# A second batch loaded as pairs of heads in six-token runs, with a recomputed order

## The chip, the cores and the metric

The kernel runs on one core of a Trainium2 chip. The metric is the device time of one execution in microseconds (us): the median of 4 runs before the change is 292.82 us, from 292.14 to 293.37. Engines are named as in the profile: PE is TensorE (PEld its weight loads), DVE VectorE, ACT ScalarE, POOL GpSimd, SP SyncE.

## What is computed

Causal attention over 8 batches and 8 heads, with 16 beacon keys in front of 576 keys, followed by a multiplicative feed-forward network over all 4,608 tokens.

```python
k_all = np.concatenate([beacon_k, k], axis=2)      # B, H, 16 + 576, 64
v_all = np.concatenate([beacon_v, v], axis=2)
scores = scale * np.matmul(q, k_all.transpose(0, 1, 3, 2))
scores = np.where(causal, -1000000000.0, scores)
a = np.exp(scores - scores.max(-1, keepdims=True))
a /= a.sum(-1, keepdims=True) + 1e-09
x = np.matmul(a, v_all)            # then tokens x (heads * 64) = 4608 x 512
out = ((x @ w1) * (x @ w2) @ w3) @ w_out    # d_ff = 1024
```

Inputs and output are float32; the kernel computes in fp16 with float32 sums.

## The kernel before

**The order.** The whole program is one string, `ORDER`: a list of small operations that a planner has put in an order for all engines at once. Each operation is a Python function of the same name (the table `ops` at the end). Every engine and every DMA queue executes its own part of the list in list order, and semaphores make it wait for what it needs. So the place of an operation in the list sets what it queues behind. The digits behind an operation are the batch, the chunk or head pair, and at the end the PSUM bank; A or D is the engine that copies, ScalarE or VectorE; P, S or A behind a load or store is the queue, POOL, SyncE or ScalarE.

**Loads.** Nearly all loads go through POOL's queue, which converts float32 to fp16 on the way: `lq`, `lk`, `lv` (q, k, v of a batch in five chunks `0` to `4` of up to 128 token rows, lines 332 and 340), `lkb`, `lvb` (beacons), `l1`, `l2` (column blocks of w1 and w2, line 390), `l3` (row blocks of w3, line 399) and `lo` (w_out, line 402). An unpaired chunk comes with tokens on partitions and heads side by side, so that every piece is one token of one head, 64 values.

Batch 0 comes otherwise (line 349): `lq 0 c` and `lk 0 c` load a *pair of heads*, `c` from 0 to 3, with six consecutive tokens on each of 96 partitions, so a piece is 6 x 64 values. Such a load lands in half of a buffer of the output staging `st8`; `cast` (line 407) moves it to `o16` in an order fit for TensorE, `tq`/`tk` (line 418) make six transposes of 96 x 96 in place of four per chunk, and `eq`/`ek` (line 437) copy the result from PSUM to `qTs`/`kTs`. The beacons of batch 0 go by way of `tn` and `en`.

**Transposing the rest.** For other batches a chunk of q or k is transposed either by TensorE (`tq`/`tk`, then `eq`/`ek`) or by a DMA transpose on SyncE's queue (`Dq` at line 471, `Dk` at line 477). Buffers of q, k, v, qT and kT exist twice, by batch number modulo 2.

**Attention.** `s b g` computes one of 13 groups of score blocks of batch b into a pair of PSUM banks (line 508). Group 0 needs the last query chunk and all keys. `exp` (ScalarE, line 518) writes them to a ring of 8 buffers; `m` masks on VectorE; `v` multiplies by the values (line 539) and `n` divides by the sums (VectorE). `x`/`ex` on TensorE, or `TX` as a DMA transpose on SyncE (line 574), put the result into `xT`.

**Feed-forward.** w3 is folded into w_out once, in the first third of the loads: `t3`, `e3`, `f`, `ew` make `Wt = w3 @ w_out`, with `t3` and `f` on TensorE (lines 484 and 493). For each of nine stretches of 512 tokens, `a` and `b` (line 580) are the products with 128 columns of w1 and w2, four matmuls each; `ea` and `eb` multiply them; `o` (line 601) are eight matmuls with `Wt`; `eo` copies and `st` stores. `a m f` needs the w1 block `f // 2`, loaded by `l1`, and `b m f` that of w2, loaded by `l2`. `spin` is idle work that keeps TensorE running.

Of the kernel before, what the change touches and what calls it, by code (L numbers as in the profile page):

```python
# [74 lines left out]
f 1 3 6; lv 1 0; ek 0 2 D 5; tk 1 0 7; ew 1 A 6; f 5 0 4; ek 1 0 D 7; l3 7; tq 0 3 5; f 5 1 4;
l2 1; eq 0 3 D 5; f 5 2 4; cast 0 2 q A; lq 1 1 P; f 5 3 4; tq 0 2 6; ew 5 A 4; lv 1 4; tk 1 1 7;
eq 0 2 D 6; ek 1 1 A 7; tk 1 2 5; l1 2; ek 1 2 D 5; s 0 6 0; s 0 7 2; lq 1 3 P; exp 0 6 0;
tq 1 4 6; v 0 1 0 7; eq 1 4 D 6; v 0 0 1 5; lk 1 4 P; n 0 1 0 7; exp 0 7 2; v 0 0 0 6; lq 1 0 P;
n 0 0 1 5; s 0 8 0; s 0 9 2; s 0 10 4; n 0 0 0 6; exp 0 8 0; lk 1 3 P; v 0 1 1 7; m 0 2 0; t3 7 6;
exp 0 9 2; m 0 2 1; l1 0; s 0 11 0; e3 7 D 6; exp 0 11 0; v 0 2 0 3; lvb 1; n 0 1 1 7; f 7 0 6;  # L80
lkb 2; tq 1 1 2; exp 0 10 4; n 0 2 0 3; s 0 12 0; f 7 1 6; m 0 3 0; f 7 2 6; m 0 3 1; eq 1 1 A 2;
lq 2 0 P; v 0 3 0 7; exp 0 12 0; v 0 2 1 5; lv 1 3; n 0 3 0 7; tq 1 3 4; tk 1 4 3; n 0 2 1 5;
x 0 0 7; eq 1 3 A 4; l1 1; v 0 3 1 2; ek 1 4 A 3; ex 0 0 D 7; f 7 3 6; lv 1 1; n 0 3 1 2; tq 1 0 7;
ew 7 A 6; tk 1 3 5; l2 0; x 0 4 4; eq 1 0 D 7; x 0 2 3; ek 1 3 A 5; x 0 3 6; ex 0 4 D 4; x 0 1 7;
ex 0 3 D 6; ex 0 2 A 3; lv 1 2; s 1 0 0; s 1 1 4; s 1 2 2; ex 0 1 D 7; exp 1 0 0; a 0 4 6; l1 3;
exp 1 1 4; m 1 0 0; l2 2; a 0 0 7; ea 0 4 D 6; l2 3; exp 1 2 2; tq 2 0 5; m 1 0 1; a 0 5 6;
# [104 lines left out]
def kernel(  # L191
# [13 lines left out]
    nc = tc.nc  # L205
# [492 lines left out]
```

## Time and profile before

| what | value |
|---|---|
| median of 4 runs | 292.82 us (292.14 to 293.37) |
| the profiled execution | 293.16 us |
| its span, first to last instruction | 291.5 us |
| TensorE clock granted | 0.999 |
| POOL's DMA queue | 114,960 packets, 26.98 MB |
| SyncE's and ScalarE's DMA queue | 40,016 packets, 11.40 MB |
| HBM read, written | 39.32 MB, 9.44 MB |
| pair load of batch 0 on POOL | 6 of them, 0.64 to 0.67 us to issue |
| chunk load of q, k or v on POOL | mean 0.86 us to issue |

How to read it: the page gives each engine's busy time and its share of the span, and then the span in 40 equal slices of 7.3 us, one digit each (9 is 90% busy or more). The row `DMA` is the mean over the core's 16 DMA engines. The *chain of waits* goes back from the last instruction, at each step to what released it. *Landing* is the moment when a DMA's data are there. Packets under 512 bytes are 145,136 of 155,214.

### The profile page before, as it was taken

What the parts mean: (1) busy time and instruction counts of PE and PEld (TensorE: products, weight loads), DVE (VectorE), ACT (ScalarE), POOL (GpSimd) and SP (SyncE); (2) the same over time, 40 slices, a digit from 0 to 9 for tenths busy, and PEclk for the clock granted to TensorE, in tenths of its full rate; (3) what the DMA queues carried; (4) which work ended last, traced back from release to release, by engine and by line L of the source; (5) the groups of instructions that cost most, each with busy time, mean ns of one, the idle gap of its engine ahead of it and who ended that gap; (6) DMA issues with size and microseconds to landing.
All of it is one profiled execution on the core that took longest, in us unless ns stands there. A gap on an engine that the chain in (4) does not pass through costs nothing.

```text
span 291.5 us, 6996 instructions
## 1 busy us (share of the span) xinstructions
PE 282.8 (97%) x2894; PEld 153.1 (53%) x2894; DVE 169.2 (58%) x366; ACT 148.6 (51%) x190; POOL 135.5 (46%) x189
## 2 busy tenths in 40 slices
PE   6999999999999999999999999999999999999995
PEld 3445674566565555565444554555555544444443
DVE  4435684874576668765573665447655566562660
ACT  3834888177926865766205573587255741002002
POOL 8768979786984752754582810591010000100000
PEclk9999999999999999999999999999999999999999
DMA  8999999999999999999999990699951111043003
GB/s 164 196 191 178 176 157 174 165 137 150 184 162 130 197 167 173 142 148 155 173 195 156 213 125 18 115 169 153 155 145 45 38 27 38 36 103 133 0 36 144
DMA packets 155214, 39.10 MB, mean 134 GB/s; under 512 B 145136, under 2 KB 151024, under 8 KB 155184
## 3 DMA queue, kind: packets, MB, share of 16 engines
q0 software_dynamic: 114960, 26.98, 106.5%
q1 hardware_dynamic: 40016, 11.40, 26.0%
q8 instruction: 22, 0.36, 0.5%
q10 hardware_dynamic: 208, 0.29, 0.4%
q14 instruction: 8, 0.07, 0.1%
HBM read 39.32 MB, written 9.44 MB: 167 GB/s over the span
## 4 chain that ended last, share of the span: by engine, by line
PE 76%; DMA 13%; POOL 7%; issue 1%; ACT 1%; SPq 0%; DVE 0%; POOLq 0%; ACTq 0%
PE one L580 40%; PE one L601 21%; PE one L539 8%; PE pair L508 7%; DMA w<-in_moe_w_dram 5%; DMA xT<-x 3%; DMA xT<-in_moe_w_dram 3%; DMA wo<-in_moe_w_out_dram 2%; POOL va L340 2%; POOL w L390 1%; ACT ring L518 1%; POOL st L357 1%; POOL q L332 1%; POOL xT L399 1%; POOL k L340 1%
## 5 line engine op out<-in xcount | busy, mean ns | idle before, releaser
L580 PE MATMUL one<-xT,w 128*128 128x512 f16 x576 | 134.6, 380 | 1.0 <-DMA w<-in_moe_w_dram 0.8
L518 ACT ACTIVATE ring<-pair 128x1024 f16<-128x1024 f32 x104 | 99.1, 1027 | 30.2 <-PE pair L508 29.8
L580 PEld LDWEIGHTS <-w 128*128 128x128 f16 x576 | 52.7, 98 | 60.1 <-issue 2.6
L601 PE MATMUL one<-Wt,gT 128*128 128x512 f16 (+1 forms) x296 | 66.5, 374 | 0.0
L595 DVE TENSOR_TENSOR gT<-one,asb 128x512 f16<-128x512 f32 x72 | 49.1, 689 | 21.8 <-PE one L580 15.0
L615 POOL DMA_DIRECT2D out_dram<-st x29 | 16.5, 569 | 92.4 <-ACT st L300 49.1
L300 ACT ACTIVATE asb<-one 128x512 f32<-128x512 f32 x36 | 21.4, 604 | 59.2 <-DVE gT L595 28.2
L601 PEld LDWEIGHTS <-gT 128*128 128x128 f16 x296 | 27.7, 98 | 31.0 <-issue 1.4
L539 PEld LDWEIGHTS <-ring 128*128 128x128 f16 x960 | 35.2, 97 | 10.3 <-issue 1.0
L340 POOL DMA_DIRECT2D va<-in_v_dram x40 | 34.2, 861 | 13.2 <-PE one L539 8.7
L539 PE MATMUL one<-va,ring 128*128 128x65 f16 x960 | 37.4, 194 | 0.2 <-DMA va<-in_v_dram 0.2
L302 DVE TENSOR_SCALAR asb<-one 128x512 f32<-128x512 f32 x36 | 24.7, 690 | 21.3 <-PE one L580 20.9
L340 POOL DMA_DIRECT2D k<-in_k_dram x35 | 29.9, 864 | 9.0 <-DMA kT<-k 8.4
L332 POOL DMA_DIRECT2D q<-in_q_dram x35 | 30.2, 866 | 5.9 <-DMA w<-in_moe_w_dram 3.4
L551 DVE TENSOR_TENSOR x<-one,rd 128x256 f16<-128x256 f32 (+1 forms) x64 | 31.4, 491 | 2.2
L508 PE MATMUL pair<-qT,kT 64*128 64x80 f16 (+4 forms) x736 | 30.4, 225 | 0.3 <-ACT ring L518 0.2
L300 ACT ACTIVATE st<-one 128x512 f32<-128x512 f32 (+1 forms) x21 | 12.2, 581 | 35.3 <-PE one L601 35.3
L508 PEld LDWEIGHTS <-kT 64*128 64x128 f16 x736 | 19.9, 95 | 14.1 <-issue 11.5
L528 DVE TENSOR_TENSOR ring<-ring,MD 128x768 f16<-128x768 f16 x32 | 17.7, 553 | 8.7 <-ACT ring L518 8.5
L550 DVE RECIPROCAL rd<-one 128x4 f32<-128x4 f32 (+1 forms) x64 | 11.8, 184 | 13.8 <-PE one L539 11.4
L302 DVE TENSOR_SCALAR st<-one 128x512 f32<-128x512 f32 x16 | 11.1, 691 | 14.3 <-PE one L601 14.3
L528 DVE TENSOR_TENSOR ring<-ring,MX 128x384 f16<-128x384 f16 x32 | 11.3, 354 | 12.8 <-ACT ring L518 12.7
(62 smaller groups left out, 131.4 us busy)
## 6 DMA issues: line engine op xcount, KB each, us to landing
out_dram<-st POOLq DMA_DIRECT2D x29, 256.0 KB, 5.1
q<-in_q_dram POOLq DMA_DIRECT2D x28, 128.0 KB, 7.7
va<-in_v_dram POOLq DMA_DIRECT2D x24, 128.0 KB, 6.7
k<-in_k_dram POOLq DMA_DIRECT2D x21, 128.0 KB, 6.6
xT<-in_moe_w_dram POOLq DMA_DIRECT2D x8, 256.0 KB, 7.4
w<-in_moe_w_dram POOLq DMA_DIRECT2D x8, 256.0 KB, 7.3
out_dram<-st SPq DMA_DIRECT2D x6, 256.0 KB, 2.0
wo<-in_moe_w_out_dram POOLq DMA_DIRECT2D x4, 256.0 KB, 6.2
```

Of the source, the lines that this page charges most:

```text
L300: nc.scalar.activation(dst, src, AF.Copy, scale=by)
L302: nc.vector.tensor_scalar(dst, src, by, None, ALU.mult)
L332: nc.gpsimd.dma_start(dst[:rows, c], src[b, :, ds(c * P, rows), :].rearrange("h s d -> s h d"))
L340: nc.gpsimd.dma_start(dst[ds(p0, rows), c], src[b, :, ds(s0, rows), :].rearrange("h s d -> s h d"))
L508: nc.tensor.matmul(shape(n, "pair")[:, hh, ds(col, w)], kT[ds(hh * 64, 64), t, ts(jt, P)], qT[ds(hh * 64, 64), t, ds(q0, w)],)
L518: nc.scalar.activation(held(b, g)[:, :, 0:GW], shape(n, "pair"), AF.Exp, scale=scale)
L528: nc.vector.tensor_tensor(blk, blk, msk, ALU.mult)
L539: nc.tensor.matmul(pv[:, 2 * at + hh, 0 : D + 1], held(b, g)[:, hh, ds(col, P)], va[:, jt, 2 * t + hh, 0 : D + 1], start=(jt == 0), stop=( ...
L551: nc.vector.tensor_tensor(x16s[b % NB2][:, ds(2 * h, ni), ts(t, P)].rearrange("p i (h d) -> p i h d", h=2), pv[:, 0 : 2 * ni, 0:D].rearran ...
L580: nc.tensor.matmul(bank(n), w12[:, kt, ds(i * DF + kf * P, P)], xT[:, kt, ds(mc * 512, 512)], start=(kt == 0), stop=(kt == NKT - 1),)
L595: nc.vector.tensor_tensor(gTs[mc % 2][:, kf, :], bank(n), asb[slot["asb", (mc, kf)]], ALU.mult)
L601: nc.tensor.matmul(bank(n)[:, 0:w], gTs[mc % 2][:, kf, ts(mt, P)], Wt[:, kf, ds(c0, w)], start=(kf == 0), stop=(kf == NFT - 1),)
```

## The change

Batch 1 is loaded like batch 0: `NPAIRED = 2` replaces the test for batch 0 in `lq`/`lk`, `lkb`, `tq`/`tk` and `eq`/`ek`. Its five chunks of q and five of k become four pair loads each; eight `cast`, one `tn` and one `en` come in. The landing places become a list of eight half buffers that are used in turn, so that each may be used a second time after the `cast` that read it. The buffers `q16s[1]` and `k16s[1]` are then first used by batch 3. The other part is a new `ORDER`, computed by the planner with longer durations for DMAs; nearly every operation changes its place. In the new order batch 2 has nine chunks transposed by TensorE and one, `Dq 2 4`, by DMA (before seven and three); one `TX` of batch 6 becomes `x`/`ex`. The casts, copies and stores are divided anew between engines and queues, three more stores going to SyncE near the end.

Of the order, the part up to the first scores of batch 2 is shown for both, and the last `TX` of the new one:

```diff
 ORDER = """
-consts 0; lk 0 0 S; lq 0 0 A; l3 3; consts 1; spin 8 7; lkb 1; lkb 0 P; l3 4; lk 0 1 P; lq 0 1 P;
-cast 0 0 k A; lo 0; consts 2; cast 0 0 q D; spin 2 7; tk 0 0 6; lo 1; tq 0 0 7; ek 0 0 A 6;
-eq 0 0 D 7; spin 1 0; t3 3 5; lvb 0; tn 0 6; lo 2; e3 3 A 5; l3 6; spin 3 7; t3 4 4; en 0 A 6;
-l3 0; s 0 0 0; s 0 1 2; e3 4 A 4; cast 0 1 k D; lk 0 3 P; tk 0 1 6; cast 0 1 q D; l3 2; exp 0 0 0;
-spin 1 7; s 0 2 4; ek 0 1 D 6; tq 0 1 7; eq 0 1 D 7; exp 0 1 2; f 4 0 6; lq 1 2 P; m 0 0 0;
-f 3 0 7; exp 0 2 4; m 0 0 1; s 0 3 0; s 0 4 2; lo 3; f 4 1 6; lv 0 2; exp 0 4 2; f 3 1 7; s 0 5 4;
-l3 1; f 4 2 6; exp 0 3 0; f 3 2 7; t3 6 3; lv 0 1; exp 0 5 4; m 0 1 0; e3 6 D 3; spin 2 0; t3 0 2;
-lk 0 2 P; m 0 1 1; f 6 0 5; e3 0 A 2; cast 0 3 k D; l3 5; f 6 1 5; tk 0 3 4; f 6 2 5; ek 0 3 A 4;
-lq 0 3 P; t3 2 3; f 0 0 2; e3 2 D 3; lv 0 4; f 0 1 2; f 0 2 2; f 2 0 4; lk 1 0 P; f 2 1 4; f 2 2 4;
-lv 0 0; f 6 3 5; f 4 3 6; ew 6 A 5; f 2 3 4; lq 0 2 P; ew 4 A 6; t3 1 5; tq 1 2 3; ew 2 A 4;
-lk 1 1 P; f 3 3 7; eq 1 2 D 3; f 0 3 2; ew 3 A 7; e3 1 D 5; lk 1 2 P; ew 0 D 2; spin 1 6; f 1 0 6;
-f 1 1 6; lq 1 4 P; cast 0 2 k D; t3 5 7; cast 0 3 q A; lv 0 3; tk 0 2 5; e3 5 D 7; f 1 2 6;
-f 1 3 6; lv 1 0; ek 0 2 D 5; tk 1 0 7; ew 1 A 6; f 5 0 4; ek 1 0 D 7; l3 7; tq 0 3 5; f 5 1 4;
-l2 1; eq 0 3 D 5; f 5 2 4; cast 0 2 q A; lq 1 1 P; f 5 3 4; tq 0 2 6; ew 5 A 4; lv 1 4; tk 1 1 7;
-eq 0 2 D 6; ek 1 1 A 7; tk 1 2 5; l1 2; ek 1 2 D 5; s 0 6 0; s 0 7 2; lq 1 3 P; exp 0 6 0;
-tq 1 4 6; v 0 1 0 7; eq 1 4 D 6; v 0 0 1 5; lk 1 4 P; n 0 1 0 7; exp 0 7 2; v 0 0 0 6; lq 1 0 P;
-n 0 0 1 5; s 0 8 0; s 0 9 2; s 0 10 4; n 0 0 0 6; exp 0 8 0; lk 1 3 P; v 0 1 1 7; m 0 2 0; t3 7 6;
-exp 0 9 2; m 0 2 1; l1 0; s 0 11 0; e3 7 D 6; exp 0 11 0; v 0 2 0 3; lvb 1; n 0 1 1 7; f 7 0 6;
-lkb 2; tq 1 1 2; exp 0 10 4; n 0 2 0 3; s 0 12 0; f 7 1 6; m 0 3 0; f 7 2 6; m 0 3 1; eq 1 1 A 2;
-lq 2 0 P; v 0 3 0 7; exp 0 12 0; v 0 2 1 5; lv 1 3; n 0 3 0 7; tq 1 3 4; tk 1 4 3; n 0 2 1 5;
-x 0 0 7; eq 1 3 A 4; l1 1; v 0 3 1 2; ek 1 4 A 3; ex 0 0 D 7; f 7 3 6; lv 1 1; n 0 3 1 2; tq 1 0 7;
-ew 7 A 6; tk 1 3 5; l2 0; x 0 4 4; eq 1 0 D 7; x 0 2 3; ek 1 3 A 5; x 0 3 6; ex 0 4 D 4; x 0 1 7;
-ex 0 3 D 6; ex 0 2 A 3; lv 1 2; s 1 0 0; s 1 1 4; s 1 2 2; ex 0 1 D 7; exp 1 0 0; a 0 4 6; l1 3;
-exp 1 1 4; m 1 0 0; l2 2; a 0 0 7; ea 0 4 D 6; l2 3; exp 1 2 2; tq 2 0 5; m 1 0 1; a 0 5 6;
-eq 2 0 D 5; lq 2 2 P; ea 0 0 A 7; s 1 3 0; s 1 4 2; s 1 5 4; ea 0 5 D 6; lk 2 0 P; exp 1 3 0;
-a 0 3 7; lk 2 2 P; exp 1 5 4; m 1 1 0; a 0 2 6; lq 2 1 P; exp 1 4 2; b 0 0 5; m 1 1 1; lq 2 4 P;
-v 1 0 0 4; eb 0 0 5; v 1 0 1 3; lq 3 4 P; n 1 0 0 4; b 0 1 2; n 1 0 1 3; v 1 1 0 5; lv 2 0;
-b 0 4 4; n 1 1 0 5; b 0 2 3; eb 0 4 4; lq 2 3 P; b 0 5 5; ea 0 2 A 6; ea 0 3 D 7; lk 2 3 P;
-eb 0 2 3; a 0 1 6; lk 2 1 P; eb 0 5 5; Dk 2 0; tq 2 2 7; a 0 6 4; lk 2 4 P; ea 0 1 A 6; eq 2 2 D 7;
-eb 0 1 2; lvb 2; tk 2 2 6; b 0 3 7; ek 2 2 A 6; lv 2 4; ea 0 6 D 4; Dq 2 4; lv 2 3; s 1 6 0;
-s 1 7 2; s 1 8 4; eb 0 3 7; exp 1 6 0; tq 2 1 6; lk 3 1 P; b 0 6 7; eq 2 1 D 6; exp 1 8 4; m 1 2 0;
-a 0 7 6; eb 0 6 7; lq 3 1 P; exp 1 7 2; v 1 2 0 5; m 1 2 1; tq 2 3 7; n 1 2 0 5; ea 0 7 A 6;
-b 0 7 4; lkb 3; eq 2 3 A 7; v 1 1 1 6; Dk 2 3; eb 0 7 4; lv 2 1; s 1 9 0; s 1 10 2; s 1 11 4;
-n 1 1 1 6; exp 1 9 0; lk 3 2 P; tk 2 1 7; tk 2 4 6; ek 2 1 D 7; exp 1 10 2; s 1 12 0; lk 3 0 P;
-ek 2 4 D 6; o 0 0 7; Dq 3 4; m 1 3 0; lk 3 4 P; exp 1 11 4; lq 3 2 P; exp 1 12 0; v 1 3 0 6;
-m 1 3 1; Dk 3 1; o 0 2 5; n 1 3 0 6; eo 0 0 A 7; st 0 0 P; Dq 3 1; x 1 4 6; v 1 3 1 7; eo 0 2 A 5;
-ex 1 4 D 6; x 1 0 4; st 0 2 P; n 1 3 1 7; v 1 2 1 6; ex 1 0 A 4; s 2 0 2; s 2 1 0; s 2 2 4;
...
+consts 0; lk 0 0 S; lq 0 0 A; l3 1; consts 1; spin 8 7; lkb 0 P; lo 0; lo 1; l3 2; l3 3;
+cast 0 0 k A; cast 0 0 q D; lq 0 1 P; consts 2; spin 2 7; tk 0 0 6; lo 2; tq 0 0 7; ek 0 0 D 6;
+eq 0 0 A 7; spin 1 0; t3 1 5; lk 0 1 P; tn 0 6; lo 3; e3 1 A 5; en 0 D 6; spin 1 7; s 0 0 0;
+s 0 1 2; s 0 2 4; l3 4; exp 0 0 0; f 1 0 7; f 1 1 7; exp 0 1 2; l3 0; m 0 0 0; exp 0 2 4; m 0 0 1;
+spin 2 6; t3 2 6; lk 0 3 P; e3 2 D 6; spin 2 0; t3 3 3; lq 0 2 P; f 2 0 6; e3 3 A 3; cast 0 1 q D;
+lk 0 2 P; f 2 1 6; tq 0 1 5; f 3 0 4; eq 0 1 A 5; l3 5; f 3 1 4; f 3 2 4; cast 0 1 k D; lv 0 2;
+tk 0 1 5; f 1 2 7; ek 0 1 D 5; f 2 2 6; lkb 1 P; f 1 3 7; f 2 3 6; ew 1 A 7; f 3 3 4; lq 0 3 P;
+ew 2 D 6; t3 4 7; ew 3 A 4; s 0 3 0; s 0 4 2; s 0 5 4; e3 4 D 7; lvb 1; exp 0 3 0; t3 0 6;
+cast 0 3 k D; l3 6; f 4 0 7; exp 0 5 4; m 0 1 0; f 4 1 7; cast 0 2 q D; lv 0 0; f 4 2 7; e3 0 A 6;
+m 0 1 1; tq 0 2 5; lv 0 3; f 4 3 7; eq 0 2 D 5; tk 0 3 4; ew 4 A 7; f 0 0 6; ek 0 3 D 4; lv 0 4;
+t3 5 5; cast 0 2 k A; f 0 1 6; e3 5 D 5; lvb 0; f 0 2 6; exp 0 4 2; lq 1 0 P; tk 0 2 7;
+cast 0 3 q D; f 0 3 6; lv 0 1; ek 0 2 A 7; tq 0 3 5; eq 0 3 D 5; ew 0 A 6; s 0 6 0; s 0 7 2; l2 1;
+exp 0 6 0; t3 6 7; lk 1 0 P; f 5 0 6; e3 6 D 7; l2 2; f 5 1 6; exp 0 7 2; tn 1 5; m 0 2 0; f 6 0 7;
+l3 7; en 1 D 5; f 6 1 7; l1 3; f 6 2 7; f 5 2 6; cast 1 0 q A; lq 1 1 P; f 5 3 6; lkb 2; f 6 3 7;
+ew 5 D 6; v 0 1 0 5; lk 1 1 P; ew 6 A 7; tq 1 0 4; n 0 1 0 5; v 0 1 1 6; eq 1 0 A 4; lk 1 2 P;
+v 0 0 0 7; n 0 1 1 6; cast 1 0 k A; lk 1 3 P; s 0 8 0; v 0 0 1 5; n 0 0 0 7; exp 0 8 0; tk 1 0 6;
+n 0 0 1 5; v 0 2 0 7; lk 2 0 P; s 0 9 2; s 0 10 0; s 0 11 4; ek 1 0 A 6; n 0 2 0 7; exp 0 9 2;
+m 0 2 1; t3 7 6; lv 1 1; e3 7 D 6; exp 0 11 4; s 0 12 2; m 0 3 0; lq 1 2 P; f 7 0 7; v 0 3 0 6;
+exp 0 10 0; m 0 3 1; l1 1; f 7 1 7; n 0 3 0 6; f 7 2 7; l2 3; exp 0 12 2; v 0 2 1 5; cast 1 1 k D;
+cast 1 1 q D; x 0 4 6; lv 1 0; cast 1 2 k D; tk 1 1 4; ex 0 4 A 6; n 0 2 1 5; tk 1 2 3; x 0 0 2;
+ek 1 1 A 4; l1 0; v 0 3 1 6; ek 1 2 D 3; cast 1 3 k A; tq 1 1 5; l1 2; f 7 3 7; n 0 3 1 6;
+eq 1 1 A 5; tk 1 3 4; lv 1 4; tk 2 0 3; ew 7 D 7; x 0 2 6; ek 1 3 A 4; lv 1 2; x 0 1 5; ex 0 2 D 6;
+s 1 0 0; ex 0 1 A 5; x 0 3 7; ek 2 0 D 3; lv 1 3; exp 1 0 0; s 1 1 4; cast 1 2 q D; ex 0 0 D 2;
+tq 1 2 6; l2 0; s 1 2 2; s 1 3 0; eq 1 2 D 6; ex 0 3 A 7; exp 1 3 0; m 1 0 0; a 0 2 7; lq 2 2 P;
+b 0 2 6; lk 2 2 P; exp 1 2 2; m 1 1 0; ea 0 2 D 7; s 1 4 0; s 1 5 2; exp 1 1 4; eb 0 2 6; lvb 2;
+a 0 0 7; exp 1 5 2; m 1 0 1; a 0 1 6; lq 2 3 P; ea 0 0 D 7; exp 1 4 0; a 0 3 5; m 1 1 1; lq 2 1 P;
+ea 0 1 D 6; b 0 3 7; lk 2 3 P; ea 0 3 D 5; v 1 0 0 6; lk 2 1 P; eb 0 3 7; s 1 6 2; s 1 7 0;
+s 1 8 4; exp 1 6 2; n 1 0 0 6; lq 1 3 P; b 0 1 7; exp 1 8 4; m 1 2 0; lk 2 4 P; b 0 0 6; eb 0 1 7;
+exp 1 7 0; lq 2 0 P; v 1 0 1 3; m 1 2 1; v 1 2 0 7; eb 0 0 6; lv 2 0; tk 2 2 5; v 1 1 1 4;
+n 1 0 1 3; ek 2 2 A 5; lkb 4; tq 2 3 6; v 1 1 0 2; n 1 2 0 7; eq 2 3 A 6; lq 2 4 P; tq 2 2 5;
+tq 2 1 3; n 1 1 1 4; lv 2 3; eq 2 2 A 5; a 0 5 6; eq 2 1 A 3; n 1 1 0 2; lq 3 1 P; tk 2 3 7;
+b 0 5 5; ea 0 5 D 6; cast 1 3 q A; lq 3 3 P; ek 2 3 D 7; a 0 6 4; eb 0 5 5; lk 3 3 P; tq 1 3 6;
+ea 0 6 A 4; tk 2 4 7; tk 2 1 5; lv 2 4; eq 1 3 D 6; tq 2 0 3; ek 2 4 A 7; a 0 4 4; lv 2 2;
+eq 2 0 D 3; ek 2 1 A 5; a 0 7 6; lv 2 1; ea 0 4 D 4; Dq 2 4; s 1 9 0; s 1 10 2; s 1 11 4; lq 4 1 P;
+ea 0 7 A 6; exp 1 9 0; b 0 7 7; lk 4 4 P; lk 3 0 P; b 0 6 6; exp 1 11 4; m 1 3 0; eb 0 7 7;
+lk 3 2 P; s 1 12 0; exp 1 10 2; eb 0 6 6; v 1 3 0 5; Dq 3 1; lk 4 0 P; b 0 4 7; m 1 3 1;
+exp 1 12 0; n 1 3 0 5; v 1 2 1 6; Dk 3 3; eb 0 4 7; s 2 0 2; s 2 1 4; s 2 2 0; exp 2 0 2;
...
+v 7 1 0 6; eb 6 6 7; o 6 1 5; n 7 1 0 6; TX 7 4; o 6 2 6; eo 6 1 A 5; TX 7 0; st 6 1 P; o 6 3 7;
+eo 6 2 D 6; st 6 2 P; o 6 0 6; eo 6 3 D 7; st 6 3 S; s 7 11 0; s 7 12 2; eo 6 0 A 6; exp 7 11 0;
+a 7 0 7; st 6 0 S; b 7 1 6; exp 7 12 2; m 7 3 1; ea 7 0 D 7; b 7 6 5; v 7 3 1 7; a 7 1 4;
+n 7 3 1 7; b 7 0 3; TX 7 1; ea 7 1 A 4; eb 7 1 6; a 7 3 7; TX 7 3; eb 7 0 3; b 7 5 6; ea 7 3 D 7;
+a 7 2 4; TX 7 2; b 7 2 7; ea 7 2 D 4; b 7 3 3; eb 7 2 7; a 7 5 4; eb 7 3 3; a 7 6 7; ea 7 5 D 4;
...
     NOWN = 2
+    NPAIRED = 2
     HELD = 2
...
     half = RUN * D
-    spare = [sts[i][:, half : 2 * half].bitcast(FP16) for i in (7, 6, 5, 4)]
-    spare += [sts[i][:, half : 2 * half].bitcast(FP16) for i in range(NOWN, 4)]
+    spare = [(i, 1) for i in (7, 6, 5, 4, 3, 2)] + [(i, 0) for i in (3, 2)]
     landed = {}
...
     def lq(b, c, e, src=q, z="q"):
-        if b == 0:
+        if b < NPAIRED:
             pair = src[b, ds(2 * c, 2)].rearrange("h (p j) d -> p h (j d)", j=RUN)
             if e in "SA":
                 land = sts[take("own", (z, c), NOWN)]
                 queue = nc.sync if e == "S" else nc.scalar
             else:
-                land, queue = spare.pop(0), nc.gpsimd
+                i, at = spare[take("spare", (z, b, c), len(spare))]
+                land = sts[i][:, ds(at * half, half)].bitcast(FP16)
+                queue = nc.gpsimd
             queue.dma_start(land[:NR].rearrange("p (h n) -> p h n", h=2), pair)
-            landed[z, c] = land
+            landed[z, b, c] = land
...
     def lkb(b, e="P"):
-        if b == 0 and e == "P":
+        if b < NPAIRED and e == "P":
...
     def cast(b, t, z, e="D"):
-        o16 = o16s[z][take("o16" + z, t, 2)]
+        o16 = o16s[z][take("o16" + z, (b, t), 2)]
         copy(
             e,
             o16[:NR].rearrange("p j (h d) -> p h j d", h=2),
-            landed[z, t][:NR].rearrange("p (h j d) -> p h j d", h=2, j=RUN),
+            landed[z, b, t][:NR].rearrange("p (h j d) -> p h j d", h=2, j=RUN),
...
     def tq(b, c, n, z="q"):
-        if b == 0:
-            o16 = o16s[z][slot["o16" + z, c]]
+        if b < NPAIRED:
+            o16 = o16s[z][slot["o16" + z, (b, c)]]
...
     def eq(b, c, e, n, z="q"):
         dst, pt = (qTs, kTs)[z == "k"][b % NB2], bank16(n)
-        if b == 0:
+        if b < NPAIRED:
```

## Prediction

> **What bounds the kernel now.** Views in this order: the page's busy shares and 40 slices, then the chain of waits for the first 72 us, then the queue of SyncE.
>
> ```profile
> span 291.5 us, 6996 instructions
> ...
> PE 282.8 (97%) x2894; PEld 153.1 (53%) x2894; DVE 169.2 (58%) x366; ACT 148.6 (51%) x190; POOL 135.5 (46%) x189
> ...
> PE   6999999999999999999999999999999999999995
> ...
> DMA  8999999999999999999999990699951111043003
> ```
>
> TensorE idles 291.5 - 282.8 = 8.7 us in all: a better order can win little, a worse one can lose more. The DMA engines are as full as TensorE for the first 24 slices, about 175 us.
>
> ```profile
> 14.56 8.51 DMA xT<-in_moe_w_dram
> ...
> 31.59 7.66 DMA w<-in_moe_w_dram
> 39.25 0.28 issue
> 39.54 0.90 POOL q L332
> ...
> 45.27 8.06 DMA w<-in_moe_w_dram
> 53.33 0.04 issue
> 53.37 3.63 PE one L580 x16
> ```
>
> Columns: start, length, what. Up to 53.33 the chain runs through loads and their issue; from there it is TensorE almost without a break. So loads pace the front and matmuls the rest. The load issued at 31.59 landed at 39.25, and the eighth issue after it began at 39.54: eight loads are in flight and POOL waits for the oldest.
>
> **A ruler for TensorE.** Busy digits hide slowing, since a matmul's modelled end stretches. I add undisturbed durations (us) from the chain and the timeline: `a`/`b` 0.86, `o` 1.73, `v` 0.37 or 0.55, one `s` group 0.23, a folding matmul pair `f` 0.43, `t3` 0.45, `x` and an unpaired `tq`/`tk` 0.22, a paired one 0.26, `tn` 0.25, a spin 0.216, the first eight 3.1. Work begins at 1.26.
>
> - Before, up to `b 0 4` (the matmul at 53.37): spins 5.3, 8 paired 2.1, 11 unpaired 2.4, 5 `x` 1.1, `tn` 0.25, `t3` 3.6, 19 `s` 4.4, 32 `f` 13.8, 11 `v` 5.0, 7 `a`/`b` 6.0; with the start 45.1. TensorE is 8.3 us behind its own work.
> - Before, up to `s 2 0`, at 71.20 in the timeline: 6 more unpaired 1.3, 2 `x` 0.4, 7 `s` 1.6, 5 `v` 2.4, 9 `a`/`b` 7.7, 2 `o` 3.5: 62.1, so 9.1 behind.
>
> **TensorE's own work** changes little. Batch 1's 10 transpose groups of four matmuls become 8 of six, with one `tn` for its beacons; batch 2 swaps two DMA transposes for two groups of four. Over the whole order: paired 8 to 16, +2.08; unpaired 17 to 9, -1.76; one `tn`, +0.25; one `x` in place of a DMA transpose, +0.22; two spins fewer, -0.43. Sum **+0.36 us**, on the path, since TensorE has nothing to hide it under.
>
> **The loads.** Spacing of landings (issue in the timeline plus time to landing), medians over the front: a 128x512-column block of w3 or w_out 1.22, of w1/w2 1.37, 128 rows of q/k/v 0.84, a short chunk 0.52, a pair of heads 0.79, a beacon 0.18. Before, the 18th POOL load landed at 23.07 and the 51st at 53.33; my spacings give 29.5 for that stretch and the trace 30.3, so I add 2.5%.
>
> The Trainium skill has a rule for this part: "DMA: Bandwidth & Descriptors", section Why small descriptors are slow, gives every packet about 3 cycles beside one per 32 B, so 256 B take 11 cycles (27% lost) and 1,536 B take 51 (6%). Rows first: 128 rows of eight heads, 256 KB read in 256 B runs, take 0.84; a pair, 288 KB read in 1,536 B runs, 0.79. Batch 1's ten loads (8 x 0.84 + 2 x 0.52 = 7.8) become eight of 0.79, 6.3: **1.5 us less DMA**. By the rule, as an estimate, the pair would take 0.84 x 288/256 x (51/48)/(11/8) = 0.73, and the gain be 1.9 us. The six pair spacings are 0.71, 0.72, 0.74, 0.83, 1.01 and 1.40; three agree with the rule, but the loads around decide too. I take the median, 1.5, and leave the rule to the fast rival.
>
> - After, the first eight loads hold one w3 and one w_out block in place of a pair and a beacon: 12.86 (where the eighth lands now: 6.80 + 6.07) + 1.47, less 0.6 for the gap that the mask instructions left in a short queue: 13.7.
> - Loads 9 to 49: 12 pairs 9.5, 6 blocks 7.3, 9 chunks 7.6, 2 short 1.0, 4 beacons 0.7, 8 blocks of w1/w2 11.0: 37.1, with 2.5% 38.0. The 49th, `l2 0`, lands at 51.7. `b 0 1` needs it, after 43.4 us of work: 8.3 behind. The saving is spent: the new order has 8 w1/w2 blocks loaded there, the old one 7, and less matmul work ahead of the point. **No gain at the gate**, uncertain by -1.8 to +1.
> - Loads 50 to 62: 8 chunks 6.7, 2 beacons, 1 pair, 2 short: 8.9; before, loads 52 to 62 took 10.2 for 9.1 by my spacings, as DMA transposes began. I take 9.5: the 62nd, `lq 2 4`, lands at 61.2.
>
> **The wait that takes over.** Of batch 2 only `Dq 2 4` still goes through a DMA transpose ahead of `s 2 0`; it is SyncE's first instruction after the opening load, so it starts when its rows land, and what queues behind it there (`Dq 3 1`, `Dk 3 3`) has 24 us to spare. Its kind in the trace (start, length, engine; below, us to landing):
>
> ```profile
> 58.66 1.18 SPq L471 DMA_TRANSPOSE qT<-q  x1
> ```
>
> ```profile
> qT<-q SPq DMA_TRANSPOSE x1, 6.4
> ```
>
> The six transposes between 56 and 69 us took 5.3 to 7.0. With 6.4 it lands at 61.2 + 0.1 + 6.4 = 67.7. TensorE's work up to `s 2 0` is now 57.7 (spins 4.8, 16 paired 4.2, 9 unpaired 2.0, `x` 1.1, `tn` 0.5, `t3` 3.6, `s` 6.0, `f` 13.8, `v` 6.8, `a`/`b` 13.8, start 1.26), so it would be there at 57.7 + 8.3 = 66.0 and waits. It leaves 10.0 behind instead of 9.1: **+0.8 us** (rounded from 9.96 - 9.15). Behind it in TensorE's queue stand all later matmuls, so nothing recovers it. In the order only 4.4 us of matmuls lie between `Dq 2 4` and `s 2 0`; the tightest such pair before, `Dk 2 3`, had 6.8.
>
> **Edits that I cost at nothing.** Eight more casts: four on ScalarE at 0.83 in batch 1, the rest on VectorE at 0.35 to 0.58; paired copies out of PSUM 0.64 (ScalarE) or 0.75 (VectorE) against 0.60 and 0.42. ScalarE was busy 12.8 of 20 us in 20:40 and 11.0 in 40:60, VectorE 11.9 and 14.1; those gaps cover them; uncovered, each cast is 0.4 to 0.8 late. POOL issues eight loads of 0.65 instead of ten of 0.87: -3.5 us of POOL, which waits for landings anyway. A landing slot is shared by two loads, the next of which waits for a cast five or more loads back: covered. The skill's page "SBUF — State Buffer", section Who interferes with whom, speaks against this part: a fast VectorE copy locks GpSimd out, descriptors included. By that rule up to 8 casts x 0.4 = 3 us of POOL. The row says otherwise: the cast of 0.36 at 9.07 lies inside two issues of 0.58 that took 1.13 together. Zero. Late waits: `TX 7 0` has 3.9 us of matmuls ahead of its reader (4.1 before) and landed in 2.4 there; zero. The last 3.1 us after the final matmul stay.
>
> **Sum.** +0.36 + 0.8 = +1.2 us. The profiled execution took 293.16 (span 291.5 and 1.66 around it), 0.34 over the median 292.82. So 294.3 on its scale, **294.0** as a median.
>
> **Rivals.**
> - *The load relief reaches the end* (faster). Pairs at 0.73 as by the rule, no 2.5%, and a 5.3 us transpose: `l2 0` at 13.7 + 37.1 - 12 x 0.06 = 50.1, 6.7 behind there, and `s 2 0` at 57.7 + 6.7 = 64.4. That is 2.45 us less lag than now, and +0.36: 290.7. For it: transposes and row loads share the engines, and there are fewer pieces. Against: spacing of pairs reached 1.4 once.
> - *The transpose comes very late* (much slower). If `lq 2 4` lands at 63.57 (56.70 + 6.87), where the 62nd load lands now, and the transpose takes 7.0, `s 2 0` starts at 70.7: 12.9 behind, +3.8 + 0.36: 297.0. It decides from a landing after 66.9 on. For it: ScalarE, VectorE, POOL and the loads are all denser in 20:60 and each can push the queue. Against: the DMA total is smaller.
> - *The new order doesn't do what it says*: durations lengthened for loads alone, so transposes stay too tight; that is the +0.8 already counted.
>
> **How the numbers follow.** What a measurement tells from no change is 0.3%, 0.9 us: 291.9 to 293.7. My forecast has 0.52, and spreads 292.8 to 295.5: slower 0.34, same 0.15, faster 0.03. The fast rival 0.24: faster 0.21, same 0.03. The late transpose 0.24: all slower. Faster 0.24, same 0.18, slower 0.58. The range 290.6 to 297.0 ends at the two rivals' times.
>
> **What would show it.** A wait of TensorE at an `s` line for `qT` of 1 to 2 us near 66 to 68; `l2 0` landing at 51 to 53; about 58 us of work up to `s 2 0`. A `qT` row without a wait, or `s 2 0` before 66.9, says the transpose step is wrong; waits on casts, that the cover was thin; new waits past 100 us, that I should not have left the rest alone.

## The result, and the profile after

| what | before | after |
|---|---|---|
| median | 292.15 us (291.05 to 294.42, 64 runs) | 293.75 us (291.92 to 295.84, 43 runs) |
| ratio to before, 95% interval | | 1.0049 (1.0036 to 1.0062) |
| profiled execution, its span | 293.16, 291.5 us | 294.14, 292.3 us |

The medians lie 1.6 us apart, in the direction and near the size forecast (+1.2). The page of the changed kernel begins so:

```profile
span 292.3 us, 7066 instructions
...
PE 283.5 (97%) x2916; PEld 154.3 (53%) x2916; DVE 177.0 (61%) x379; ACT 148.0 (51%) x187; POOL 130.5 (45%) x184
...
PE   8899889998999999999999999999999999999995
...
DMA  7999999999999999999999990999825004300033
```

TensorE is busy 0.7 us longer and its idle time is still 8.8 us (292.3 less 283.5), but the row of digits shows that it lies elsewhere: less in the first slice, and 8s in slices 2, 5, 6 and 10 (7 to 15, 29 to 44 and 66 to 73 us), where the kernel before had 9s. VectorE has 7.8 us more to do, POOL 5.0 us less. The chain of waits, columns start, length and what, shows both new gaps:

```profile
31.63 7.30 DMA st<-in_k_dram
38.93 0.02 issue
38.95 0.63 DVE o16k L297
39.58 0.05 issue
39.63 0.43 PE one L424 x6
...
60.24 7.20 DMA qT<-q
67.44 0.04 issue
67.48 0.79 PE pair L510 x20
```

The second gap is the forecast one: `Dq 2 4` started when its rows landed, and the scores of batch 2, of which two matmuls had run at 66.34, went on when it had. The first was not in the forecast: the paired k of batch 1 (`lk 1 2`) lands at 38.93, VectorE casts it, and `tk 1 2` follows. TensorE's waits in the first 72 us (columns: total, times, longest) give both the same weight:

```profile
PE one L424 <- DVE o16k L297: 0.9, 1, 0.9
PE pair L510 <- DMA qT<-q: 0.9, 1, 0.9
PE one L424 <- ACT o16k L297: 0.5, 2, 0.3
```

**Only the front moves.** Ten profiled executions of the new order, edited or not, took 224.63 to 224.72 us from the start of `s 2 1` to the end, whatever had happened ahead of it (spans 290.1 to 293.3). Two executions of the order before took 220.27 and 220.03 us from its first scores of batch 2. So what these executions of one order differ by lies ahead of those scores, in the first 69 to 71 us. I read them with the prediction's ruler: the start of an operation in the timeline, less TensorE's own undisturbed work up to it. This is its *lag*; an operation is "8 behind" when its lag is 8 us. Not all lag is waiting, since the ruler leaves something out (last section). A *gate* is an arrival that decides when TensorE can go on.

### The profile page after: what moved, and what is told of

It is laid out like the page before. It is cut to its first block, busy times and chain, and to the rows that moved or that the text cites. A ratio compares the mean times of both kernels' runs of the same rounds, so it can differ in the third digit from the quotient of the medians.

```text
span 292.3 us, 7066 instructions
## 1 busy us (share of the span) xinstructions
PE 283.5 (97%) x2916; PEld 154.3 (53%) x2916; DVE 177.0 (61%) x379; ACT 148.0 (51%) x187; POOL 130.5 (45%) x184
## 4 chain that ended last, share of the span: by engine, by line
PE 85%; DMA 9%; POOL 2%; DVE 2%; ACT 1%; issue 1%; POOLq 0%; DVEq 0%; ACTq 0%
PE one L582 42%; PE one L603 22%; PE one L541 9%; PE pair L510 7%; DMA xT<-in_moe_w_dram 3%; DMA st<-in_k_dram 2%; DMA qT<-q 2%; PE one L495 2%; DMA va<-in_v_dram 2%; PE one L567 1%; PE one L424 1%; PE one L486 1%; PE one L430 0%; POOL xT L401 0%; POOL wo L404 0%
## 5 line engine op out<-in xcount | busy, mean ns | idle before, releaser
L582 PE MATMUL one<-xT,w 128*128 128x512 f16 x576 | 132.8, 380 | 0.2
L603 PE MATMUL one<-Wt,gT 128*128 128x512 f16 (+1 forms) x296 | 65.8, 374 | 0.0
L301 ACT ACTIVATE asb<-one 128x512 f32<-128x512 f32 x32 | 19.1, 598 | 79.0 <-PE one L582 65.9
L617 POOL DMA_DIRECT2D out_dram<-st x26 | 14.8, 568 | 70.4 <-ACT st L301 38.4
L541 PE MATMUL one<-va,ring 128*128 128x65 f16 x960 | 38.2, 194 | 0.6 <-DVE asb L303 0.2
L303 DVE TENSOR_SCALAR asb<-one 128x512 f32<-128x512 f32 x40 | 27.6, 690 | 12.0 <-PE one L582 11.3
L303 DVE TENSOR_SCALAR st<-one 128x512 f32<-128x512 f32 x23 | 15.9, 691 | 30.9 <-PE one L603 30.9
L340 POOL DMA_DIRECT2D k<-in_k_dram x30 | 25.7, 870 | 3.8 <-DMA kT<-k 2.7
L332 POOL DMA_DIRECT2D q<-in_q_dram x30 | 25.8, 864 | 2.5 <-DMA q<-in_q_dram 0.8
L301 ACT ACTIVATE st<-one 128x512 f32<-128x512 f32 (+1 forms) x14 | 8.0, 568 | 28.6 <-PE one L603 27.4
L530 DVE TENSOR_TENSOR ring<-ring,MX 128x384 f16<-128x384 f16 x32 | 11.3, 354 | 16.2 <-ACT ring L520 16.0
```

Source lines behind the costliest of these rows:

```text
L301: nc.scalar.activation(dst, src, AF.Copy, scale=by)
L303: nc.vector.tensor_scalar(dst, src, by, None, ALU.mult)
L332: nc.gpsimd.dma_start(dst[:rows, c], src[b, :, ds(c * P, rows), :].rearrange("h s d -> s h d"))
L340: nc.gpsimd.dma_start(dst[ds(p0, rows), c], src[b, :, ds(s0, rows), :].rearrange("h s d -> s h d"))
L530: nc.vector.tensor_tensor(blk, blk, msk, ALU.mult)
L541: nc.tensor.matmul(pv[:, 2 * at + hh, 0 : D + 1], held(b, g)[:, hh, ds(col, P)], va[:, jt, 2 * t + hh, 0 : D + 1], start=(jt == 0), stop=( ...
```

## The experiments

All kernels compute everything. The ratio is to the kernel before, on the same chip. Four questions were asked: is the wait for `Dq 2 4` the cost; is the pairing; is the w2 block `l2 0`; is it the order of all loads.

**1. The transposed chunk.** Chunk 4 of batch 2's q goes through TensorE instead:

```diff
-Dq 2 4; s 1 9 0;
+tq 2 4 7; eq 2 4 D 7; s 1 9 0;
```

> The changed kernel with Dq 2 4 replaced by tq 2 4 and eq 2 4 on TensorE and VectorE, ahead of s 1 9. Theory (the DMA transpose is the one wait that the change adds): s 2 1 no longer waits for 67.4 but starts near 66.6; 1.1 us of wait go, 0.22 us of TensorE work come: 0.85 us faster than the changed kernel, 292.9 on the scale where before is 292.15 (ratio to before 1.0025). Rival (the front is late by its loads and casts anyway, the wait only moves to the next reader): no change, 293.75, ratio 1.005.

Measured: 293.57 us (9 runs), 1.0064 (1.0039 to 1.0088). The `qT` row is gone from TensorE's waits and `s 2 1` is 8.8 behind instead of 9.7, yet the median is that of the changed kernel within 0.2 us.

The same wait, taken away and made longer by the place of the load alone:

```diff
-eb 0 0 6; lv 2 0;
+eb 0 0 6; lq 2 4 P; lv 2 0;
...
-eq 2 3 A 6; lq 2 4 P; tq 2 2 5;
+eq 2 3 A 6; tq 2 2 5;
```

> The changed kernel with lq 2 4 issued two places earlier on POOL, ahead of lv 2 0 and lkb 4, which nobody needs before 70 us. Theory: its rows land 0.95 us earlier, Dq 2 4 starts and lands as much earlier (66.5 instead of 67.4), TensorE's wait at s 2 1 shrinks from 0.9 to nearly 0: 0.9 us faster than the changed kernel, 292.85, ratio to before 1.0024. Rival (the transpose's end is set by how full the DMA engines are, not by its start): it still lands near 67.4, 293.75, ratio 1.005.

Measured: 293.73 us (14 runs), 1.0045 (1.0025 to 1.0066). The `qT` wait is gone, the time is not. In its profile TensorE waited 0.8 us for a w block instead, ahead of the scores.

```diff
-eq 2 3 A 6; lq 2 4 P; tq 2 2 5;
+eq 2 3 A 6; tq 2 2 5;
...
-lq 3 1 P; tk 2 3 7;
+lq 3 1 P; lq 2 4 P; tk 2 3 7;
```

> The changed kernel with lq 2 4 issued two places later on POOL, behind lv 2 3 and lq 3 1. Theory: rows 1.6 us later, s 2 1 waits 2.5 instead of 0.9 us: 295.3, ratio to before 1.0108. Rival (the transpose's place is not what costs): 293.75, ratio 1.005.

Measured: 295.22 us (4 runs), 1.0111 (1.0081 to 1.014). The chain of this kernel:

```profile
62.29 6.16 DMA qT<-q
68.44 0.04 issue
68.48 0.80 PE pair L510 x20
```

Rows two loads later cost 1.5 us, rows two loads earlier gain nothing. So the transpose is a real gate, but it closes only just behind another one.

**2. The pairing alone, in the order of before.** `NPAIRED = 2` with the old order; batch 1's ten loads became eight, and each group took the place of an unpaired one:

```diff
-tk 1 1 7; eq 0 2 D 6; ek 1 1 A 7; tk 1 2 5; ek 1 2 D 5;
+cast 1 1 k D; eq 0 2 D 6; cast 1 2 k D;
...
-exp 0 6 0; tq 1 4 6;
+exp 0 6 0; tk 1 1 7; ek 1 1 A 7; tk 1 2 5; ek 1 2 D 5; cast 1 1 q D;
...
```

> Batch 1 in pairs of heads as in the change, but in the order of before: eight pair loads stand in the places of the ten chunk loads, casts ahead of the transposes, the beacons by tn and en. Theory of the prediction (pairing saves 1.5 us of DMA ahead of b 0 4, which was the gate; the new order spends it): b 0 4 runs 1.2 to 1.5 us earlier, TensorE has 0.13 us more work, and nothing later waits: 291.0, ratio to before 0.996. Rival (the pairing costs as much as it saves: casts, wider copies out of PSUM, and a landing-to-transpose way that is 0.5 us longer in an order that had 0.05 us of slack): 292.2 to 293, ratio 1.000 to 1.003, the new order then no worse than the pairing.

Measured: 295.71 us (6 runs), 1.0122 (1.0088 to 1.0155): 3.6 us slower than before, although eight loads replace ten. TensorE's waits of this kernel:

```profile
PE pair L511 <- DVE qT L298: 0.9, 1, 0.9
PE one L542 <- ACT kT L298: 0.8, 1, 0.8
PE one L425 <- DVE o16k L298: 0.7, 2, 0.5
```

None of these is a load. TensorE waits for copies out of PSUM and for casts, at places where the old order had hundredths of a microsecond to spare (`lk 1 2` landed 0.05 us ahead of its use). The cast is a step between landing and transpose that the unpaired load does not have; a new order is needed to hide it, so that both halves of the change belong together.

**3. How far one execution can be trusted.** Both kernels once more, unchanged.

> The kernel of before, unchanged, for a second trace, since its profiled execution (293.16) lay 1.0 us above its median (292.15). Theory (executions differ in the front, where loads set the pace): whatever this execution's time, the part after s 2 0 takes the same 220.3 us (291.5 - 71.2) within 0.3, and s 2 0 itself moves with the time; at a time near the median s 2 0 starts near 70.2, 8.1 us behind TensorE's own work. Rival (executions differ all along): the part after s 2 0 changes by as much as the time.

> The changed kernel, unchanged, for a second trace. Theory: the part from s 2 1 to the end takes 224.7 us (292.3 - 67.65) within 0.3 again; the front's loads land within 0.5 us of the first trace, and TensorE is 8.1 to 8.9 us behind its own work at b 0 1. Rival: the later part differs.

Measured: 291.76 (span 290.0) and 294.81 us (span 293.1), against 293.16 and 294.14 in the first profiles. The first profile of the kernel before was a late one: its `s 2 0` was 9.15 behind, here 7.95. The prediction took its reference there. The chain of the changed kernel, and its waits for casts:

```profile
31.18 8.95 DMA st<-in_k_dram
40.15 0.36 DVE o16k L297
40.51 0.27 DVE o16q L297
40.77 0.64 DVE o16k L297
41.46 0.43 PE one L424 x6
```

```profile
PE one L424 <- ACT o16k L297: 1.4, 2, 0.9
...
PE one L424 <- DVE o16k L297: 1.1, 2, 0.7
```

Here `lk 1 1` took 8.95 us to land, three casts followed one another, and TensorE was already so late (8.74 behind at `tk 1 2`) that the `qT` wait did not appear at all. That is one reason why removing it gains so little: here the first gate covered it. The other is that the 7.20 us of the first profile were the longest of six (last section); here the transpose started at 61.93, took 5.0 and had landed 1.2 us before `s 2 0` started at 68.18.

**4. The w2 block.** In the changed kernel `l2 0` landed at 51.40, and `b 0 1` followed at 51.57. `l1 2`, which is read 8 us after it lands, was put behind it:

```diff
-l1 2;
...
-l2 0;
+l2 0; l1 2;
```

> The changed kernel with l1 2, which is read at 56 us, issued behind l2 0 instead of four places ahead of it, so that l2 0 lands one w1/w2 block (1.35 us) earlier. Theory (two gates in series, l2 0 for b 0 1 and Dq 2 4 for s 2 0): b 0 1 runs up to 1.2 us earlier, but the rows of lq 2 4 still land at 60, s 2 1 still starts near 67.4 and waits longer: no gain, 293.7, ratio to before 1.005. Rival (the front's gate at b 0 1 alone makes the loss): 1.2 us gained, 292.5, ratio 1.0015.

> The changed kernel with both: l1 2 behind l2 0, and chunk 4 of batch 2's q transposed by tq 2 4 and eq 2 4 on TensorE and VectorE. Theory (two gates in series; each alone gives little because the other follows): the 1.2 us of the first gate now reach s 2 0, less what the chunks of batch 2 hold back, together 1.0 to 1.5 us: 292.3 to 292.8, ratio 1.001 to 1.003. Rival (the front is slow by its casts and copies, not by these two): as the changed kernel, 293.5 or more, ratio 1.005.

Measured: 293.81 us (9 runs), 1.0042 (1.001 to 1.0073), and with the edit of experiment 1 on top 293.88 us (12 runs), 1.0058 (1.0037 to 1.0079). The second is a miss, and so is the first in its reason: `l2 0` now landed 1.25 us ahead of its use, and `b 0 1` was where it had been (51.64). TensorE came late to it; most of its lag had been made by `tk 1 2` (6.8 of 8.2).

**5. The order of all loads.** Ahead of batch 1's k the queue holds `l2 1`, `l2 2` and `l1 3`, 1.3 to 1.5 us each, whose data lay 14, 24 and 22 us unread. They, `l2 3` and `l1 2` (five blocks of 256 KB, where the expectation says four and 128) were moved close to their use:

```diff
-l2 1; ... l2 2; ... l1 3; ... l2 3; ... l1 2;
...
-l2 3;
+l2 1;
...
-lk 2 2 P;
+lk 2 2 P; l1 2;
...
-lq 2 1 P;
+lq 2 1 P; l2 2; l1 3;
...
-lq 2 0 P;
+lq 2 0 P; l2 3;
```

> The changed kernel with four 128 KB-wide blocks of w1 and w2 loaded later: l2 1 where l2 3 stood, and l1 2, l2 2, l1 3, l2 3 behind the first loads of batch 2, close to their first use (56 to 62 us). Dq 2 4 stays. Theory (the front is paced by the order of the loads, and the paired k of batch 1 queues behind blocks that are needed 20 us later): t3 7 6 and tk 1 2 come about 2.5 us earlier, with 1.5 to 2.5 us less lag there, but lq 2 4 is still the 62nd load and lands near 60, so that Dq 2 4 holds the scores of batch 2 until about 67.4: the wait for qT grows to some 2 us and the time stays at 293.3 to 293.8. Rival (casts and copies on VectorE and ScalarE pace the front, loads only follow): tk 1 2 and b 0 1 at most 0.5 us earlier, no growth of the qT wait, 293.7. Second rival (the blocks collide with the loads of batch 2, whose slack was 0.9 to 1.2 us): 294.5 or more.

Measured: 293.59 us (12 runs), 1.005 (1.0025 to 1.0075), no change, as the theory had it. `lk 1 2` landed at 35.51, 2.9 us ahead of `tk 1 2`; then the other gate took all of it back:

```profile
50.63 7.25 DMA st<-in_q_dram
57.91 0.84 ACT o16q L297
58.79 0.43 PE one L424 x6
...
62.06 5.78 DMA qT<-q
67.89 0.80 PE pair L510 x20
```

`Dq 2 4` starts at 62.06 because its rows are still the 62nd load. The other cast of the chain, `cast 1 3 q`, waits for a load that now has blocks in front of it: 1.0 us of TensorE that had not been there.

Both gates taken away, with `lvb 2`, `lv 2 0` and `lkb 4` moved behind `lq 2 4` as well (shown against `blocks_behind`):

```diff
-Dq 2 4;
+tq 2 4 7; eq 2 4 D 7;
...
-lq 2 4 P;
+lq 2 4 P; lvb 2; lv 2 0; lkb 4;
```

> As blocks_behind, and chunk 4 of batch 2's q transposed by TensorE instead of by DMA, with lvb 2, lv 2 0 and lkb 4 behind lq 2 4. Both gates are then gone. Theory: the lag at the first scores of batch 2 falls from 8.7 to 10 us to 6.5 to 7.5, they start near 65.2, and the time is 291.2 to 292.2, two below the changed kernel and at or under the kernel before. Rival (casts and copies pace the front): b 0 1 still past 51, 293.4 to 293.8. Second rival (loads of batch 2 become the gate at once): 292.8 to 293.4.

Measured: 292.54 us (22 runs), 1.0003 (0.9986 to 1.002). That is 1.2 us under the changed kernel and 1.05 under `blocks_behind` in the same session; against the kernel before it cannot be told from no change. The time is above the 291.2 to 292.2 that the theory gave: moved loads and the chunk on TensorE together take back most of the 1.6 us, but not all. No run has the first two edits without the three loads behind `lq 2 4`, so their share isn't known. The chain of `blocks_and_tensor` holds no DMA from 20 to 72 us; what is left are round trips between TensorE and the copying engines:

```profile
33.84 0.57 PE one L486 x8
34.50 0.70 DVE gT L297
35.25 0.61 PE one L495 x2
...
41.58 0.59 DVE o16q L297
42.22 0.43 PE one L424 x6
```

How many microseconds TensorE stood behind its own work, by the ruler, in one execution each (all but `blocks_and_tensor` and `tensor_chunk` have 0.22 us less of work in all):

| at | changed kernel | again | tensor_chunk | blocks_behind | blocks_and_tensor |
|---|---|---|---|---|---|
| `t3 6 7` | 3.7 | 4.3 | 3.9 | 4.3 | 4.0 |
| `t3 7 6` | 5.1 | 6.6 | 6.1 | 4.8 | 4.4 |
| `tk 1 2` | 6.9 | 8.7 | 7.0 | 5.7 | 5.5 |
| `a 0 2` | 7.8 | 9.6 | 7.8 | 6.6 | 6.4 |
| `b 0 1` | 8.1 | 10.0 | 8.4 | 6.9 | 6.9 |
| `s 2 1` | 9.7 | 10.5 | 8.8 | 10.1 | 7.3 |
| its time less its kernel's median | +0.4 | +1.1 | -0.2 | +0.8 | -0.7 |

The last row warns: `blocks_behind` is seen in a late execution, `blocks_and_tensor` in an early one. The first two columns part just ahead of `t3 7`, at `tk 1 0`: its pair `lk 1 0`, queued behind `l2 1`, landed at 31.81 and 33.22, the cast followed, and TensorE waited 0.35 and 0.89 us. They part again at `tk 1 1` and `tk 1 2`. With `l2 1` out of the way (last two columns) there is no wait at `tk 1 0` and less than 0.2 at `tk 1 2`: loads. The step of 0.8 from `tk 1 2` to `a 0 2` is in every column, loads early or late: not loads. Nor is it waiting: TensorE idles for 0.1 us in it, and six changes to and from score groups, which the ruler leaves out, make up an estimated 0.6.

**6. What is left.** Two last runs. In the first, ScalarE's cast of the k pair goes two places up, into a gap of 0.54 us:

```diff
-cast 1 3 k A; tq 1 1 5;
+tq 1 1 5;
...
-ex 0 4 A 6;
+cast 1 3 k A; ex 0 4 A 6;
```

> As blocks_and_tensor, and ScalarE's cast of the paired k of batch 1 (cast 1 3 k, 0.84 us) two places earlier in its queue, ahead of ex 0 4, where ScalarE idled 0.54 us and the pair has landed 3 us before. Theory (with the loads early, what is left of the rise in lag from 4.4 at t3 7 to 6.9 at b 0 1 is ScalarE's queue, full from 38 to 43): a 0 2 starts 0.3 to 0.5 us earlier in lag, and the time is 292.0 to 292.3, against 292.5 without it. Rival (TensorE waits there for its own results in turn, by a copy and back, whoever copies): a 0 2 unmoved, 292.5; or tk 1 1 and ex 0 4 come later by what the cast takes, 292.7.

Measured: 292.52 us (22 runs), 1.001 (0.9998 to 1.0022), no gain. The copy `ex 0 4` came behind the cast and TensorE waited 0.4 us for that; `s 1 0` was 6.0 behind instead of 5.6. One place in a queue was traded for another. In the second the same cure is tried on the kernel before, unpaired, by moving eight loads that lay 5 to 22 us unread:

```diff
-l2 1; ... lv 1 0; ... lv 1 4; ... l1 3; ... l2 3; ... lkb 2; ... lq 3 4 P; ... lv 2 0;
...
-lv 1 2; ... l2 2; ... lq 2 2 P; ... lk 2 2 P; ... lq 2 4 P; ... lk 2 4 P;
+lv 1 2; lv 1 0; lv 1 4; ... l2 2; l2 1; ... lq 2 2 P; lkb 2; ... lk 2 2 P; l1 3;
+lq 2 4 P; l2 3; ... lk 2 4 P; lq 3 4 P; lv 2 0;
```

> The kernel before, batch 1 unpaired, with the loads alone moved in POOL's queue: l2 1, lv 1 0, lv 1 4, l1 3, l2 3, lkb 2, lq 3 4 and lv 2 0, whose data lay 5 to 20 us unread, go behind the loads that TensorE waited for (lk 1 3, l2 0, l2 2, lk 2 3). Theory (the order of the loads paces the front of both kernels): l2 0 lands near 47.5 in place of 49 to 50, the lag at b 0 4 falls from 7.1 to 8.3 to about 6.3, s 2 0 starts near 69, and the time is 291.0 to 291.7, faster than the kernel before and than any in pairs so far: the old order then needs the pairs for nothing. Rival (copies and exponentials on ScalarE and VectorE pace the front of the old order, where the loads waited no more than 1 us): 292.0 to 292.4, no change.

Measured: 292.01 us (22 runs), 0.9988 (0.9971 to 1.0004); the kernel before had 292.27 beside it. The lag at `b 0 4` fell to 6.4 as expected, but in an execution of 291.02 us, 1.0 below the median, and the median did not reach the expected 291.7: 0.3 us lower than before, not told from no change. In the old order the cure is not shown to be worth anything. Its median is the lowest of the edited kernels, but no run shows that it beats the kernel before.

## Why the prediction was near, and which step was wrong

**TensorE's own work, +0.36:** holds past 70 us. From `s 2 0` of the old order and `s 2 1` of the new on, the lag of both grows by the same 6.3 us (15.45 less 9.15, 15.96 less 9.69), so nothing there is part of the answer, and no new waits past 100 us came. That growth is hardly waiting (0.4 to 0.6 us of idle TensorE) but what the ruler leaves out. For the whole the sum may be too small: the page has TensorE busy for 283.5 us in both executions of the changed kernel, against 282.8 and 282.3 before, 0.7 to 1.2 more. A matmul that is slowed counts as busy, so how much of this is work stays open.

**The loads to `l2 0`:** the landing was forecast at 51.7 and came at 51.40, with `b 0 1` 8.1 behind against 8.3. Batch 1's eight paired loads took 6.1 us of landings against the 6.3 of the sum. As an arrival the step was right; as a gate it was not, and this is the first step that failed. Experiment 4 moved `l2 0` and nothing followed. Most of the lag at `b 0 1` (6.9 of 8.1) had been made 12 us before, up to `tk 1 0` and `tk 1 2`, by loads queued behind w blocks that nobody read yet. I had asked only whether the 49th load came in time, not which of the 48 ahead of it TensorE waited for.

**The wait that takes over, +0.8:** found where it was put. Rows forecast for 61.2 landed at 60.15, the transpose forecast at 6.4 took 7.2, and the two errors cancelled: 67.44 against 67.7. `s 2 1` was 9.7 behind against 10.0. That was luck as well: in the second execution of the same kernel the transpose took 5.0 and TensorE did not wait for it. And the size of the wait was taken as its worth. Without it the median is lower by 0.2 us (experiment 1, with 0.22 us of work added to TensorE), because the front gate is nearly as late, and in the second execution later. Neither gate alone was worth a measurable gain; both together, with the three loads moved in that run, 1.2 us.

**Edits that I cost at nothing** is the other step that failed: "Eight more casts", "those gaps cover them". The rows for 20 to 40 us of the windows view show how the gaps shrank, first the kernel before, then the changed one (columns: stretch, its length, then busy time and instructions of PE, PEld, DVE, ACT and POOL, the clock, DMA share, GB/s):

```profile
20.00:40.00 20.00, 19.30 (x263) 12.14 (x261) 11.93 (x29) 12.79 (x17) 16.52 (x22) 1.00 1.91 176
```

```profile
20.00:40.00 20.00, 18.03 (x269) 11.54 (x268) 13.49 (x33) 16.18 (x22) 16.63 (x24) 1.00 1.59 177
```

ScalarE went from 12.8 to 16.2 of 20 us while TensorE lost 1.3; casts are 1.4 of ScalarE's 3.4, the rest the new order moved there. TensorE waited 1.3 us for the added casts in the first execution and 2.0 in the second (0.35 and 0.94; 0.89, 0.66 and 0.47). The remainder of the waits for casts shown above, 0.2 and 0.5, stands at batch 0's first cast, where the kernel before waited too, and longer:

```profile
PE one L422 <- ACT o16k L296: 1.0, 1, 1.0
```

Part of each such wait is the landing: at `tk 1 2` TensorE stood idle from 38.69, the pair landed at 38.93 and the cast took the rest. Gaps of a total size do not cover a cast that lies on the way from a late landing to a transpose; there it adds its length, 0.35 to 0.83 us. Where the pair lands early they do: in `blocks_and_tensor` TensorE waited 0.3 us for the added casts. So the zero failed together with the order of the loads, not by itself. Also wrong was the zero for VectorE beside POOL; see the last section.

**The size.** The medians differ by 1.6: 0.36 of own work by the ruler, and what is left, 1.2, of lag ahead of batch 2's scores, where the sum had 0.8. The four profiled executions only bracket that lag, between 0.5 (9.69 less 9.15) and 2.5 (10.45 less 7.95). The reference for that 0.8 came from a late execution of the kernel before (9.15; 7.95 in the next). A typical start is about 0.5 to 1 lower, by the profiled 293.16 against the median 292.15. Had I taken it, the same sum would have said some 2 us.

**The rivals.** The fast one needed cheaper loads to reach the end. Pairs did land cheaper, 0.69 us apart in the median of all 14 against 0.79 in the sum, near the 0.73 that the prediction estimated from the rule of the Trainium skill ("DMA: Bandwidth & Descriptors", Why small descriptors are slow), but the saving went into w blocks loaded early. The very late transpose is what `load_later` shows at a smaller size: 295.2.

**Open.** With the loads early, TensorE still falls 2.5 us behind between `t3 7 6` and `b 0 1`. Only 0.8 of it is idle TensorE (busy for 15.77 of these 16.55 us), and some 1.2 is an estimate for 12 changes to and from score groups at 0.1. The chain puts the idle part on copies and casts of ScalarE and VectorE; how much would be there without the casts, no run tells, and `cast_in_gap` did not reduce it. Nor is it settled whether pairs pay for batch 1 when both orders are equally well made: the best with them is 292.52 (`cast_in_gap`) and the best without 292.01, in the same session, and TensorE's added work by the ruler, 0.58, is as large as the difference.

## What to carry to other kernels

When two waits lie one behind the other on the same engine, their lengths in one profile are not what each is worth: remove both before judging either. Ask of every queue not whether the awaited load is in time, but which loads ahead of it are read much later. And price a step that is put between a late landing and its reader at its full length, since idle time elsewhere on its engine does not hide it.

## What the runs showed of the hardware

**A cast on VectorE is held by POOL's issue of a DMA.** VectorE and then POOL in the timeline of the changed kernel (start, length, engine):

```profile
38.95 0.62 DVE L297 COPY o16k<-st 96x768 f16<-96x768 f16 x1 [0.70 <-DMA st<-in_k_dram]
```

```profile
38.55 0.84 POOL L340 DMA_DIRECT2D va<-in_v_dram  x1
39.38 0.76 POOL L392 DMA_DIRECT2D w<-in_moe_w_dram  x1
```

The cast normally takes 0.35 us. This one ended at 39.57, 0.18 after the issue that it overlapped at its start, and lies on the chain. Of 128 such casts in all the profiles here, 44 took 0.40 to 0.83. The 14 in the first 6 us convert from float32. The other 30 all ended 0.15 to 0.19 us after the end of a POOL issue. The 29 that lay wholly inside one issue took 0.36 in the median. POOL's issues were not visibly longer. The row that the prediction weighed, a cast of 0.36 inside two issues, was a lucky one. The Trainium skill, "SBUF — State Buffer", section Who interferes with whom, has POOL and a VectorE copy that uses the port pair they share lock each other out for a whole instruction, by whoever issued first. The direction fits, and the price was VectorE's, not POOL's; but POOL held the cast only near the end of an issue, not for the whole of it.

**A DMA transpose of the same 80 rows** took 7.2 and 5.0 us to land in the two executions of the changed kernel, and 4.9, 5.3, 5.8 and 6.2 in four edited ones, beside row loads.

**A change between score groups and other matmuls costs TensorE about 0.1 us**, which the ruler leaves out. In the changed kernel eight `a`/`b` matmuls took 1.73 us when a transpose followed (57.13 to 58.86) and 1.82 when a score group did (59.71 to 61.53). In all the profiles here one `a` or `b` took 0.86 in the median ahead of another and 0.96 ahead of a score group.

**Single loads come late now and then.** `lk 1 1` landed 0.68 us after the load ahead of it in one execution of the changed kernel and 2.07 in the next, `lk 1 2` 1.59 and then 0.38. The profiled executions of one kernel differ in such delays of the front and not past it, and the times of one kernel spread over 3 to 4 us.
